# Loading v in f32 and narrowing it on chip, with a state update in two VectorE operations

## The chip, the cores and the metric

The kernel runs on one core of a Trainium2 chip. The metric is device time in microseconds (us) of a whole execution. Every experiment was run beside the kernel before on the same chip, in alternating rounds. The span of a profile is one execution and lies about 1.8 us under the time of the same run, so times are compared with times and spans with spans.

## The reference

A gated linear attention over 768 tokens (4 batches, 8 heads, 48 dimensions a head) is followed by a two-layer network with GELU:

```python
for t in range(S):                                   # S = 768
    state = alpha[:, :, t, :, None] * state + np.einsum('bhd,bhe->bhde', k[:, :, t], v[:, :, t])
    y[:, :, t] = np.einsum('bhd,bhde->bhe', q[:, :, t], state)
...
x = y.transpose(0, 2, 1, 3).reshape(B * S, H * D)    # 3072 x 384
out = gelu_tanh(x @ w_in) @ w_out                    # 384 x 2048, 2048 x 384
```

## The kernel before

It cuts the tokens into 6 chunks of 128 and works on *pairs*: one chunk of two batches, 12 pairs in all, numbered 0 to 11. For each pair it loads alpha (`a`), `q`, `k` and `v`. It takes the logarithm of alpha (`la`) and cumulative sums on TensorE (`cum`), scales q and k with exponentials of the sums (`qp`, `kp`), forms the attention products within the chunk (`at`), masks them (`atm`), multiplies them with v (`yps`), adds what the carried state gives, and updates the state (`kv`, `st`). Layer one (`hT`), GELU (`gT`) and layer two (`acc`) of earlier pairs fill TensorE in between.

v is narrowed to bf16 *by the load*, which GpSimd issues:

```python
def load(self, n, c, i, lo=0, hi=2):
    ...
        u[n] = self.tile(n, [C, 2, H, D], BF16 if n == "v" else F32)
        src = self.src[n][2 * i + lo:2 * i + hi].rearrange("b h s d -> s (b h) d")[c * C:(c + 1) * C]
        (nc.sync if e == "SP" else nc.gpsimd).dma_start(u[n][:, lo:hi]..., src)
```

The state is kept in pairs of heads, 128 partitions by 96 columns, of which two blocks of 64 by 48 are used. It is updated block by block:

```python
def carry(self, u, i, c, b):
    kv, old, new = u["kv", i], self.state[b][c % 2], self.state[b][(c + 1) % 2]
    for o in range(2):                                       # 64 partitions at a time
        ps, fs = slice(64 * o, 64 * o + 64), slice(D * o, D * o + D)
        acc = kv[ps, :, fs]
        if c > 0:
            ...
            nc.vector.tensor_tensor(s[ps], acc, old[ps, :, fs], op=ALU.add)
            acc = s[ps]
        nc.vector.tensor_tensor(new[ps, :, fs], acc, u["bend"][ps, i, :, None].to_broadcast(...), op=ALU.mult)
```

The order of the instructions on each engine is *planned* in Python when the kernel is built: every piece of work has a cost in a table `W`, a priority and dependencies, and a list scheduler fixes the order. Each engine then works through its list in order. Some entries of `W` stand for the time that a load takes to land. The first two pairs' alpha and q and the first pair's k go in small pieces over SyncE's and ScalarE's queues, the rest over GpSimd's:

```python
LOADS = ('gatea0', 'v0', 'gatek0', 'in 0', 'pk1', 'in 1', 'in 2', 'v1', 'in 3', 'out 0', 'out 1', '2a', ...)
RINGS = (..., ('a', 1, 0, 'SP'), ('a', 1, 1, 'SP'), ('a', 1, 2, 'SP'), ('a', 1, 3, 'SP'), ('q', 1, 0, 'SP'), ...)
```

A "gate" is a tiny GpSimd copy that waits for a piece, so that what follows in that queue starts later.

## Time and profile before

| | before |
|---|---|
| time, median of the runs ahead of the prediction | 185.78 us (184.66 to 186.07) |
| span of the profile | 183.2 us |
| TensorE, VectorE, ScalarE, GpSimd busy | 175.7, 104.2, 135.6, 60.9 us |
| first matmul of layer one | 17.2 us |

In this timeline the columns are start, duration, engine, line, operation, operands and count, and in brackets the idle time of the engine just before and what ended it:

```profile
10.64 0.66 PE L424 MATMUL at<-qkT 64*128 64x128 bf16 x16
11.11 2.48 DVE L431 TENSOR_TENSOR atm<-at,ut 128x512 bf16<-128x512 f32 x4 [0.82 <-PE at L424]
...
11.45 0.94 ACT L301 ACTIVATE la<-a 128x384 f16<-128x384 f32 x2 [0.76 <-DMA a<-in_alpha_dram]
12.02 0.82 PE L288 MATMUL cum<-la,ut_blk 128*128 128x384 f16 x7 [0.72 <-ACT la L301]
...
13.54 0.36 PE L473 MATMUL yps<-v,atm 128*128 128x48 bf16 x8
```

TensorE does pair 0's attention products (10.64 us) *before* it stops for pair 1's sums (12.02 us), which wait for alpha of pair 1.

### The profile page before, as it was taken

The page shows a single profiled execution, that of the slowest core. Times are in us where ns is not written, and L with a number is a line of the kernel's source. Part 1 is how long each engine was busy: PE and PEld are TensorE (multiplying, and loading weights), DVE is VectorE, ACT ScalarE, POOL GpSimd, SP SyncE. Part 2 cuts the span into 40 slices and gives each one's busy share as a digit, 9 for nine tenths or more (in the row PEclk, how much of TensorE's full clock was granted, in tenths as well). Part 3 has the DMA queues.
Part 4 walks back from the last instruction along what each step waited for, and adds up shares of the span by engine and source line. Part 5 has one row for each costly group of instructions (what it writes and reads, how often), then busy time and mean ns, then how long its engine had stood idle before and what let it go on. Part 6 is the DMA issues. An engine that isn't in the chain of part 4 may idle for free.

```text
span 183.2 us, 4630 instructions
## 1 busy us (share of the span) xinstructions
PE 175.7 (96%) x1861; PEld 129.3 (71%) x1861; DVE 104.2 (57%) x232; ACT 135.6 (74%) x310; POOL 60.9 (33%) x68
## 2 busy tenths in 40 slices
PE   7887999999999999999999999999999999999993
PEld 2465869666686787687688769678677677686873
DVE  7775954065969896597499798298644715000000
ACT  3666969873888789859799768899789884491941
POOL 2595837975545755564750200000000000000000
PEclk9999999999999999999999999999999999999999
DMA  5999999999999999999999955753271290311102
GB/s 155 187 242 211 187 231 214 204 202 174 195 281 183 169 229 197 181 225 205 180 213 235 179 171 100 104 115 67 52 170 46 43 202 4 88 43 47 43 0 86
DMA packets 51206, 27.76 MB, mean 151 GB/s; under 512 B 38833, under 2 KB 48241, under 8 KB 51185
## 3 DMA queue, kind: packets, MB, share of 16 engines
q0 software_dynamic: 32096, 17.70, 69.0%
q1 hardware_dynamic: 18512, 9.38, 21.5%
q10 hardware_dynamic: 576, 0.39, 0.7%
q8 instruction: 14, 0.23, 0.6%
q14 instruction: 8, 0.06, 0.1%
HBM read 25.17 MB, written 4.72 MB: 163 GB/s over the span
## 4 chain that ended last, share of the span: by engine, by line
PE 85%; DMA 6%; ACT 3%; DVE 2%; SPq 1%; ACTq 1%; issue 0%
PE acc L516 34%; PE hT L497 31%; PE at L424 4%; PE qkT_ps L364 4%; PE yps L473 3%; DMA a<-in_alpha_dram 2%; PE yps L470 2%; DMA q<-in_q_dram 2%; PE cum L320 2%; PE kv L441 2%; DMA qkT<-kp 2%; PE xT_ps L487 1%; DVE atm L431 1%; ACT L503 1%; PE cum L322 1%; SPq L247 1%
## 5 line engine op out<-in xcount | busy, mean ns | idle before, releaser
L497 PE MATMUL hT<-xT,w_in 128*128 128x256 bf16 x576 | 70.1, 273 | 0.4 <-ACT gT L503 0.4
L503 ACT ACTIVATE gT<-hT 128x256 bf16<-128x256 f32 x192 | 63.4, 387 | 8.6 <-PE hT L497 8.3
L516 PE MATMUL acc<-w_out,gT 128*128 128x384 bf16 (+1 forms) x400 | 68.8, 319 | 0.0
L497 PEld LDWEIGHTS <-w_in 128*128 128x128 bf16 x576 | 54.0, 98 | 8.0 <-issue 0.6
L516 PEld LDWEIGHTS <-gT 128*128 128x128 bf16 x400 | 36.8, 98 | 19.6
L431 DVE TENSOR_TENSOR atm<-at,ut 128x512 bf16<-128x512 f32 x48 | 30.9, 685 | 15.0 <-PE at L424 14.5
L354 DVE TENSOR_TENSOR qp<-q,b 128x768 bf16<-128x768 f32 (+1 forms) x15 | 11.7, 794 | 18.7 <-ACT b L343 15.8
L528 ACT COPY ot<-acc 128x384 f32<-128x384 f32 (+1 forms) x18 | 8.3, 462 | 13.9 <-PE acc L516 12.6
L235 POOL DMA_DIRECT2D v<-in_v_dram x13 | 14.6, 1123 | 9.6 <-PE hT L497 2.9
L235 POOL DMA_DIRECT2D k<-in_k_dram x11 | 12.2, 1112 | 11.0 <-DVE kp L354 5.2
L343 ACT ACTIVATE b<-cum 128x768 bf16<-128x768 f32 (+1 forms) x15 | 10.2, 684 | 6.7 <-PE cum L322 3.1
L235 POOL DMA_DIRECT2D q<-in_q_dram x11 | 12.3, 1114 | 7.0 <-DMA k<-in_k_dram 1.8
L235 POOL DMA_DIRECT2D a<-in_alpha_dram x11 | 12.3, 1114 | 5.9 <-ACT gT L503 2.2
L213 ACT ACT_TABLE_LOAD x9 | 11.5, 1283 | 2.8 <-issue 2.6
L480 ACT CAST x<-yps 128x384 bf16<-128x384 f32 x16 | 7.7, 481 | 7.8 <-PE yps L473 7.6
L458 DVE TENSOR_TENSOR st<-stmp,bend 64x192 bf16<-64x192 f32 x32 | 11.3, 353 | 1.5
L354 DVE TENSOR_TENSOR kp<-k,binv 128x768 bf16<-128x768 f32 (+1 forms) x15 | 11.8, 792 | 0.2
L456 DVE TENSOR_TENSOR stmp<-kv,st 64x192 f32<-64x192 f32 x32 | 11.3, 352 | 1.0 <-PE kv L441 0.7
L503 ACT ACT_TABLE_LOAD x9 | 11.5, 1283 | 0.2
L222 PE MATMUL idle<-zero 128*128 128x512 bf16 x27 | 9.5, 462 | 1.2 <-DVE blk L778 1.2
L382 DVE COPY qkT<-qkT_ps 128x1024 bf16<-128x1024 bf16 (+1 forms) x13 | 8.7, 688 | 3.0 <-PE qkT_ps L364 2.9
L343 ACT ACTIVATE binv<-cum 128x768 bf16<-128x768 f32 (+1 forms) x15 | 10.1, 683 | 0.0
(62 smaller groups left out, 159.4 us busy)
## 6 DMA issues: line engine op xcount, KB each, us to landing
out_dram<-ot SPq DMA_DIRECT2D x23, 192.0 KB, 2.3
a<-in_alpha_dram POOLq DMA_DIRECT2D x9, 384.0 KB, 13.1
q<-in_q_dram POOLq DMA_DIRECT2D x9, 384.0 KB, 13.2
k<-in_k_dram POOLq DMA_DIRECT2D x9, 384.0 KB, 13.3
v<-in_v_dram POOLq DMA_DIRECT2D x11, 192.0 KB, 13.3
w_in<-in_moe_w_in_dram POOLq DMA_DIRECT2D x4, 384.0 KB, 7.7
w_out<-in_moe_w_out_dram POOLq DMA_DIRECT2D x4, 384.0 KB, 9.8
a<-in_alpha_dram SPq DMA_DIRECT2D x6, 96.0 KB, 3.4
```

What stands on the lines that cost most here:

```text
L213: nc.scalar.add_instruction(mybir.InstLoadActFuncSet(name=nc.get_next_instruction_name(), act_func_set_id=i, engine=mybir.EngineType.Activ ...
L222: self.nc.tensor.matmul(ps, self.zero[:, 0:self.C], self.zero, start=True, stop=True)
L235: (nc.sync if e == "SP" else nc.gpsimd).dma_start(u[n][:, lo:hi].rearrange("t b h d -> t (b h) d"), src)
L343: self.nc.scalar.activation(u[n].rearrange("t i h d -> t i (h d)")[:, lo:hi], cum, AF.Exp, scale=1.0 if n == "b" else -1.0)
L354: self.nc.vector.tensor_tensor(out, rows, b, op=ALU.mult)
L382: self.copy(e)(t, ps)
L431: self.nc.vector.tensor_tensor(u["atm", i][:, o], u["at", i][o], self.ut[:, None, :].to_broadcast([self.C, self.H // 2, self.C]), op=ALU.mult)
L456: nc.vector.tensor_tensor(s[ps], acc, old[ps, :, fs], op=ALU.add)
L458: nc.vector.tensor_tensor(new[ps, :, fs], acc, u["bend"][ps, i, :, None].to_broadcast([64, H // 2, D]), op=ALU.mult)
L497: self.nc.tensor.matmul(h, self.w_in[:, j, nt * self.C:(nt + 1) * self.C], self.xT[c][:, j, lo:hi].rearrange("p g t -> p (g t)"), start=j ...
L503: return lambda e: self.nc.scalar.activation(self.gT[c % self.NG][:, nt, lo * self.C:hi * self.C], f.pop(("h", c, lo, nt)), AF.Gelu_apprx_ ...
L516: self.nc.tensor.matmul(f["acc", c, b][:, lo:hi], self.gT[c % self.NG][:, nt, b * self.C:(b + 1) * self.C], self.w_out[:, nt, lo:hi], star ...
```

## The change

Its intent: spare VectorE four instructions per update by doing two on all 128 partitions, with a decay that is zero outside the used blocks (one tiny multiply per pair makes it, `ends`). And take the narrowing of v out of the DMA engines, where it moves in 96-byte packets: v comes in f32, and GpSimd narrows it, VectorE for the first two pairs. The core of the diff:

```diff
-    qk2=910, ..., st=1400, st0=700, ...
+    qk2=910, ..., st=1090, st0=545, end=110, ...
-    ... cast=1500, ..., cast_0=1300, share=1200, cast_1=1900, ...
+    ... early_0=1000, share=1000, early_1=1400, vb1=300, vb2=550, vb1_pool=600, vb2_pool=950, ...
-    BUFS = dict(..., ot=6, bend=8, a=4, q=4, k=4, v=6)
+    BUFS = dict(..., ot=5, bend=3, ends=8, a=4, q=4, k=4, v=3, vb=4)
 ...
-                u[n] = self.tile(n, [C, 2, H, D], BF16 if n == "v" else F32)
+                u[n] = self.tile(n, [C, 2, H, D], F32)
 ...
+    def narrow(self, u, lo, hi):
+            ... (gpsimd or vector).tensor_copy(u["vb"][:, lo:hi], u["v"][:, lo:hi])
 ...
+            acc, old, new = u["kv", i], self.state[b][c % 2], self.state[b][(c + 1) % 2]
+            if c > 0:
+                nc.vector.tensor_tensor(s, acc, old, op=ALU.add)          # 128 x 384
+                acc = s
+            nc.vector.tensor_tensor(new, acc, ends, op=ALU.mult)          # 128 x 384
 ...
+                narrow[lo:hi] = [s.add("vb", {"DVE": W[f"vb{n}"]} if early else {"POOL": W[f"vb{n}_pool"]}, P + 9 if early else -1, ...)
```

Because the cost table changed, the whole order is planned anew as well.

More of the change, by code (lines that the diff above doesn't have):

```diff
@@ L17 @@
     cum=530, cum_packed=1500, t8=450, t4=225, attn=340, kv=170, inter=170, intra=205, tx=168, l1_4=655, l1_2=340, l2=655,
-    qk2=910, qk1=500, ev8=650, ev4=350, mask=640, st=1400, st0=700, xc=520, xe=330, ot=540,
+    qk2=910, qk1=500, ev8=650, ev4=350, mask=640, st=1090, st0=545, end=110, xc=520, xe=330, ot=540,
     ev8_act=960, ev4_act=520, xc_act=450, xe_act=450, ot_act=450,
-    strip=2120, cast=1500, weight=2080, dma=2100, issue=1100, wissue=760, sp=100, store=2600, turn=1250, landed=2200, xbar_qk=1500, xbar_x=1000, late_x=2500, piece=330, late_k=1500, piece_issue=450, begin=2700, cast_0=1300, share=1200, cast_1=1900, ln_packed=1040, cold=380, fill=216, zero=1100,
+    strip=2120, weight=2080, dma=2100, issue=1100, wissue=760, sp=100, store=2600, turn=1250, landed=2200, xbar_qk=1500, xbar_x=1000, late_x=2500, piece=330, late_k=1500, piece_issue=450, begin=2700, early_0=1000, share=1000, early_1=1400, vb1=300, vb2=550, vb1_pool=600, vb2_pool=950, ln_packed=1040, cold=380, fill=216, zero=1100,
 )
@@ L156 @@
     URGENT = (2,)
-    BUFS = dict(ca=1, yk=2, ff=4, la=3, qp=4, kp=4, b8=2, kn=2, qkT=4, atm=6, x=3, ot=6, bend=8,
-                a=4, q=4, k=4, v=6)
+    BUFS = dict(ca=1, yk=2, ff=4, la=3, qp=4, kp=4, b8=2, kn=2, qkT=4, atm=6, x=3, ot=5, bend=3, ends=8,
+                a=4, q=4, k=4, v=3, vb=4)
     def __init__(self, ctx, tc, q, k, v, alpha, w_in, w_out, out):
@@ L182, in __init__ @@
         self.ident = const.tile([C, C], BF16, name="ident")
+        self.half = const.tile([C, 2], F32, name="half")
         self.ones = const.tile([C, 1], F16, name="ones")
@@ L345, in exp, with emit @@
         return emit
+    def narrow(self, u, lo, hi):
+        def emit(e):
+            if "vb" not in u:
+                u["vb"] = self.tile("vb", [self.C, 2, self.H, self.D], BF16)
+            (self.nc.gpsimd.tensor_copy if e == "POOL" else self.nc.vector.tensor_copy)(u["vb"][:, lo:hi].rearrange("t b h d -> t (b h d)"), u["v"][:, lo:hi].rearrange("t b h d -> t (b h d)"))
+        return emit
     def scaled(self, u, n, lo, hi):
@@ L441, in emit, with ends @@
                 nc.tensor.matmul(kv[:, p, :], u["kn" if u["packed"] else "kp"][:, i, 2 * p:2 * p + 2, :].rearrange("t h d -> t (h d)"),
-                                 u["v"][:, i, 2 * p:2 * p + 2, :].rearrange("t h d -> t (h d)"),
+                                 u["vb"][:, i, 2 * p:2 * p + 2, :].rearrange("t h d -> t (h d)"),
                                  start=True, stop=True)
+        return emit
+    def ends(self, u):
+        C, H = self.C, self.H
+        def emit(e):
+            t = u["ends"] = self.tile("ends", [C, 2, H // 2, 2], F32)
+            (self.nc.gpsimd if e == "POOL" else self.nc.vector).tensor_tensor(
+                t.rearrange("f i p o -> f (i p) o"), u["bend"].rearrange("f i p -> f (i p)")[:, :, None].to_broadcast([C, H, 2]),
+                self.half[:, None, :].to_broadcast([C, H, 2]), op=ALU.mult)
         return emit
@@ L449, in emit @@
         def emit(e):
-            kv, old, new = u["kv", i], self.state[b][c % 2], self.state[b][(c + 1) % 2]
-            for o in range(2):
-                ps, fs = slice(64 * o, 64 * o + 64), slice(D * o, D * o + D)
-                acc = kv[ps, :, fs]
-                if c > 0:
-                    s = self.sb.tile([C, H // 2, D], F32, tag=f"stmp{o}", bufs=2, name="stmp")
-                    nc.vector.tensor_tensor(s[ps], acc, old[ps, :, fs], op=ALU.add)
-                    acc = s[ps]
-                nc.vector.tensor_tensor(new[ps, :, fs], acc,
-                                        u["bend"][ps, i, :, None].to_broadcast([64, H // 2, D]), op=ALU.mult)
+            acc, old, new = u["kv", i], self.state[b][c % 2], self.state[b][(c + 1) % 2]
+            if c > 0:
+                s = self.sb.tile([C, H // 2, 2 * D], F32, tag="stmp", bufs=2, name="stmp")
+                nc.vector.tensor_tensor(s, acc, old, op=ALU.add)
+                acc = s
+            ends = u["ends"][:, i].rearrange("f p o -> f (p o)")[:, :, None].to_broadcast([C, H, D])
+            nc.vector.tensor_tensor(new.rearrange("f p (o d) -> f (p o) d", o=2),
+                                    acc.rearrange("f p (o d) -> f (p o) d", o=2), ends, op=ALU.mult)
         return emit
@@ L472, in emit @@
             for h in range(H):
-                nc.tensor.matmul(y[:, h, :], u["atm", i][:, h % 2, h // 2, :], u["v"][:, i, h, :],
+                nc.tensor.matmul(y[:, h, :], u["atm", i][:, h % 2, h // 2, :], u["vb"][:, i, h, :],
                                  start=c == 0, stop=True, skip_group_check=True)
@@ L548, in load @@
             nonlocal n
-            land = W[{"v": "cast", "w": "weight"}.get(key[0], "strip")]
-            loads[key] = s.add("load", {"POOL": cost}, n, emit, gate, land=W[f"cast_{key[1]}"] if key[0] == "v" and key[1] in self.PACKED else land * 3 // 8 if key[0] != "w" and key[1] in self.SPLIT else land,
+            land = W[{"w": "weight"}.get(key[0], "strip")]
+            loads[key] = s.add("load", {"POOL": cost}, n, emit, gate, land=W[f"early_{key[1]}"] if key[0] == "v" and key[1] in self.PACKED else land * 3 // 8 if key[0] != "w" and key[1] in self.SPLIT else land,
                                late=W["share"] if key[:2] == ("v", 0) else 0)
@@ L599, in tasks @@
             early = m in self.EARLY
-            lns[m], ends[m], qp, kp, be = [], [], [None, None], [None, None], [None, None]
+            lns[m], ends[m], qp, kp, be = [], [], [None, None], [None, None], []
             cums, exps = [], []
@@ L611, in tasks @@
                 if u["sums"]:
-                    be[lo:hi] = [x[2]] * n
+                    be.append(x[2])
                 ends[m].append(x[-1])
@@ L644, in tasks @@
                 owner = every[0]
+            if u["sums"]:
+                end = s.add("end", {"DVE": W["end"]}, P + 16, self.ends(u), be)
+            narrow = [None, None]
+            for lo, hi in ((0, 1), (1, 2)) if early else self.parts(m):
+                n = hi - lo
+                narrow[lo:hi] = [s.add("vb", {"DVE": W[f"vb{n}"]} if early else {"POOL": W[f"vb{n}_pool"]}, P + 9 if early else -1, self.narrow(u, lo, hi),
+                                       [loads["v", m, lo]])] * n
+            loads["v", m, 0].take("v", *narrow)
             for j in range(2):
@@ L670, in tasks @@
                 y = s.add("y", {"PE": W["intra"] + (W["inter"] if c else 0)}, P + 20 + j, self.y(u, j, c, b),
-                          ms + turned + [loads["v", m, j]] + ([states[b, c - 1]] if c else []))
+                          ms + turned + [narrow[j]] + ([states[b, c - 1]] if c else []))
                 xc = s.add("x", {"ACT": W["xc_act"], "DVE": W["xc"]}, P + 20 + j, self.x(u, j), [y])
@@ L692, in tasks @@
                         backs.append(tb)
-                    kv = s.add("kv", {"PE": W["kv"]}, P + 30 + j, self.kv(u, j), [k, loads["v", m, j]])
+                    kv = s.add("kv", {"PE": W["kv"]}, P + 30 + j, self.kv(u, j), [k, narrow[j]])
                     st = states[b, c] = s.add("st", {"DVE": W["st" if c else "st0"]}, P + 30 + j, self.carry(u, j, c, b),
-                                              [kv, be[j]] + ([states[b, c - 1], ys[b, c - 1]] if c else []))
+                                              [kv, end] + ([states[b, c - 1], ys[b, c - 1]] if c else []))
                     kv.take("yk", st)
@@ L710, in tasks @@
             kp[0].take("kp", *tq, *kvs)
-            loads["v", m, 0].take("v", *vs)
+            narrow[0].take("vb", *vs)
             if u["sums"]:
-                be[0].take("bend", *cs)
+                be[0].take("bend", end)
+                end.take("ends", *cs)
         n = 0
@@ L778, in run @@
         nc.vector.memset(self.blk, 0.0)
+        nc.vector.memset(self.half, 0.0)
+        for o in range(2):
+            nc.vector.memset(self.half[64 * o:64 * o + 64, o:o + 1], 1.0)
         for t in self.ut_blk:
```

## The prediction

> **What bounds the kernel now.** I read the page's busy times first, then the busy tenths by slice, then windows, then the chain of waits, and last the groups.
>
> ```profile
> PE 175.7 (96%) x1861; PEld 129.3 (71%) x1861; DVE 104.2 (57%) x232; ACT 135.6 (74%) x310; POOL 60.9 (33%) x68
> ...
> PE   7887999999999999999999999999999999999993
> ...
> DMA  5999999999999999999999955753271290311102
> ...
> q0 software_dynamic: 32096, 17.70, 69.0%
> ```
>
> TensorE is busy 96% of the span, VectorE 57%, GpSimd 33%. The TensorE row is full from slice 5 on, the DMA row from slice 2 to 23: after the start TensorE looks like the bound, before it the loads. The windows (us, then busy us and count of PE, PEld, DVE, ACT, POOL; granted clock, DMA share, GB/s) give it by stage:
>
> ```profile
> 0.00:30.00 30.00, 26.01 (x278) 17.66 (x279) 21.33 (x71) 19.43 (x49) 18.70 (x31) 1.00 1.23 200
> 30.00:110.00 80.00, 79.60 (x901) 59.21 (x900) 56.06 (x115) 64.58 (x139) 42.22 (x37) 1.00 1.33 203
> 110.00:180.00 70.00, 69.85 (x691) 52.44 (x686) 26.85 (x48) 51.24 (x122) 0.00 (x0) 1.00 0.35 76
> ```
>
> Busy is not full speed, so I checked the rhythm. In the chain of waits 42 matmuls of layer one take 4.58 us (109 ns each) and 16 of layer two 2.60 us (162 ns each):
>
> ```profile
> 6.94 4.41 DMA a<-in_alpha_dram
> 11.34 0.02 issue
> ...
> 28.68 4.58 PE hT L497 x42
> 33.27 2.60 PE acc L516 x16
> ```
>
> Giving every matmul the median distance from its start to the next of its kind, I sum 155.4 us of wanted work, 7.1 us of filler on zeros and 16.3 us of gaps. Of fillers and gaps together (23.4 us) about 13.6 lie before 30 us and 9.9 after; 3.2 us follow the last matmul start. After 30 us only three gaps exceed 150 ns beyond that rhythm, 1.0 us in all, the largest 0.56 us beside a table load of ScalarE; the rest is switching between kinds of matmul. So after 30 us no load and no VectorE wait costs more than about 1 us. What can be won lies in the first 30 us.
>
> There the chain runs through transfers. The last piece of alpha of pair 1 lands at 11.34 us; the logarithm, the cumulative sums and the exponentials follow. The chain then goes to VectorE's multiply of q at 15.38 us, which the waits put down to a ScalarE copy that this multiply does not read. The trace has the last q piece of pair 1 landing at 15.26 us, so I take that as what held it. Behind it on VectorE are the copies of the turned x, and the first layer-one matmul starts at 17.21 us. The first v (issued 5.06 us) lands at 12.08 us, while these alpha and q pieces are under way.
>
> The groups that the change touches:
>
> ```profile
> L458 DVE TENSOR_TENSOR st<-stmp,bend 64x192 bf16<-64x192 f32 x32 | 11.3, 353 | 1.5
> L456 DVE TENSOR_TENSOR stmp<-kv,st 64x192 f32<-64x192 f32 x32 | 11.3, 352 | 1.0 <-PE kv L441 0.7
> ...
> L458 DVE TENSOR_TENSOR st<-kv,bend 64x192 bf16<-64x192 f32 x8 | 2.8, 355 | 0.8 <-ACT gT L503 0.7
> ...
> v<-in_v_dram POOLq DMA_DIRECT2D x11, 192.0 KB, 13.3
> ```
>
> They are VectorE work with almost no idle time before it, and nothing on TensorE waits long for it: the longest total of TensorE's weight loads behind stmp is 0.9 us in four waits.
>
> **What the Trainium skill says.** (1) "VectorE: DVE Perf Modes", section "The TRN2 errata", gives (N+151)/0.96 ns for an f32 tensor_tensor. For N=192 that is 357 ns (trace 352 to 355), for 384 it is 557 (the kp multiply 128x384: 552), for 768 it is 957 (952). It agrees, so the time follows the free size and half the partitions save nothing. (2) "GPSIMD Engine Reference", section "Elementwise — side-by-side cycle accounting", gives 1.03 cycles an element for a port-bound loop, at 1.2 GHz; the trace has only a one-element copy, 0.27 us at most, so a copy of 768 is estimated at 0.27+0.66=0.93 us, which no run here shows yet. (3) "SBUF — State Buffer", section "Who interferes with whom": a VectorE instruction with two SBUF inputs contends with a GpSimd instruction that reads SBUF. The trace before has no long GpSimd read to show it. (4) "DMA: Bandwidth & Descriptors", section "Queues, rings and completion order": each DMA engine alternates between queues by packets. The trace agrees at least that the two queues slow each other: the four alpha pieces of pair 0 land 0.2 to 0.7 us apart, those of pair 1, with v under way, 0.5 to 1.5.
>
> **The change part by part.**
>
> State update. Removed: 32+32+8 VectorE instructions of 64x192, 22.6+2.8=25.4 us. Added: 16 updates of two instructions 128x384 and 4 of one, at 552 ns: 36 x 0.552 = 19.9 us. Saved 5.5 us. Added too: one tiny multiply per pair for the masked decays (16 outputs, 0.17 us by the formula), 10 of them, 1.7 us, and about 0.2 us of memsets. Net 3.6 us less on VectorE. What the path sees: next to nothing, since TensorE is full where 16 of the 20 updates lie. I give it 0.1 us.
>
> Narrowing. VectorE gets four copies of 128x384 in the first two pairs; at two elements a cycle (384/2+150)/0.96 = 356 ns, 1.4 us in all. GpSimd gets nine copies of 768 and two of 384, about 9 x 0.93 + 2 x 0.6 = 9.6 us, on an engine busy 60.9 us, so about 70. VectorE's total should be 104.2 - 3.6 + 1.4 = 102. The copies of pair 0 stand near its four masks (11.1 to 13.6 us), before an idle stretch of 1.78 us; those of pair 1 fall in the busiest part. I charge 0.3 us to the path.
>
> The load. Bytes read from HBM stay; those written for v double, 2.36 MB more (27.76 to 30.1). Two opposite effects. Where the GpSimd queue is full the landings are 2.05 to 2.15 us after the one before for a, q and k, and about 1.45 (1.4 to 1.8) for v. An f32 v will take 2.1: 0.65 us more per pair, 6.5 us over pairs 2 to 11. But from pair 4 on alpha lands 9 us and more before its logarithm (pair 5: 57.1 against 72.4 us), so this is hidden; only pair 3, whose alpha lands at 40.19 us just as it is used, is close, and TensorE has other work then (9.8 of 10 us filled from 30 to 40).
> The other effect is in the packets. The narrowed v makes 24,576 packets of 96 B at 31 ns mean, 2048 per pair: 2048 x 31 / 16 = 4.0 us of every engine. f32 strips on the same queue travel in packets of about 4 KB, some 100 per strip, at 323 ns: 100 x 323 / 16 = 2.0 us. Packets therefore fall by 24,576 - 12 x 100 to about 27,800, and q0's share by some 24 us of 183, from 69% to about 56%. In the first 15 us this should let v0 and the q pieces beside it land 0.5 to 1.5 us earlier. I count 1.0 us, of which 0.2 is taken back by v1 standing ahead of the last quarter of w_in.
>
> Sum: -0.1 + 0.3 - 0.8 = -0.6 us, and another -0.3 us as a choice, for the smaller DMA occupancy next to weights and pair 2. 185.78 - 0.9 = 184.9.
>
> **The rivals.** First, VectorE is what matters, and 3.6 us less of it shortens the end, to about 182. Its slices reach 9 in places, and it has 8.7 of 10 us busy in 60 to 70; against it, TensorE has under 1 us of gaps there, most of it switching.
> Second, the loads become the bound between 20 and 45 us: v's extra 0.65 us for pairs 1 to 3 plus weights queued behind, 186.5 to 187. For it speak the full DMA row and pair 3's alpha; against it, only 0.15 us of TensorE gaps from 30 to 40.
> Third, GpSimd becomes a gate: its queue is in order, a narrowing that waits for its v (about 13 us from issue to landing) holds back the load issues behind it, and v has three buffers in place of six. If the planned order misses the landings, loads slip by a microsecond or two a pair: harmless while 9 us ahead, 187 to 189 if it happens at pairs 2 to 4.
> Fourth, the order that the kernel plans for itself is recomputed with other costs, so instructions move on every engine; that alone may shift the time a microsecond either way.
>
> **Range and chances.** Central 184.9 us. If the early win is the full 2 us: 183. If narrowings lie on the chain and the loads slip: 187. The range is 183.0 to 187.0. Faster by over 2% needs 182.1, more than I can find in the start: 0.07. Slower by over 2% needs 189.5, a gate early on GpSimd: 0.06. Within 2%: 0.87.
>
> **What would show it.** Right: TensorE still 96% or more; VectorE near 102 us; state instructions at 552 ns; packets near 27,800 and 30.1 MB; v landing about 2.1 us after its predecessor; GpSimd copies near 0.93 us; the first layer-one matmul near 16.4 us instead of 17.2, and the end earlier by about as much. Wrong: the same start but an earlier end (VectorE mattered); GpSimd long in wait on v with loads issued late; gaps on TensorE between 30 and 60 us behind loads or behind a narrowed v; a first matmul later than 17.2 us because the copies delay the masks or the x.

## The result, and the profile after

The changed kernel took 190.59 us (median of 4 runs, 189.12 to 191.15) against 185.22 us before (184.31 to 186.07). The ratio is 1.0276 with a 95% interval of 1.0204 to 1.0347: slower, and outside the predicted range of 183.0 to 187.0. Ratios here are the mean time of one kernel's fast runs over that of the other's fast runs of the same rounds, so not quite the ratio of the medians. The span of the profile grew from 183.2 to 189.4 us, by 6.2 us. The page of the changed kernel:

```profile
PE 178.2 (94%) x1864; PEld 130.3 (69%) x1864; DVE 105.2 (56%) x218; ACT 133.6 (71%) x305; POOL 69.1 (36%) x79
...
PE   7829999999899999999999999998999999999993
...
PEclk9996999999999999999999999999999999999999
...
DMA packets 27781, 30.11 MB, mean 159 GB/s; under 512 B 14256, under 2 KB 23664, under 8 KB 27760
...
q0 software_dynamic: 8672, 20.06, 47.6%
```

Packets, bytes and GpSimd are as predicted (27,800, 30.1 MB, about 70 us). The share of q0, the queue of GpSimd's loads, fell from 69.0 to 47.6% and not to the predicted 56; it is 62.6% in carry_only, a run told of below that keeps the old load of v, so part of the fall is not v's. But the third slice of TensorE, 9.5 to 14.2 us, has fallen from 8 to 2, and the granted clock (the share of TensorE's full clock that the profile shows) in the slice after it is 0.6. The windows, in the columns of the prediction:

```profile
0.00:30.00 30.00, 24.28 (x243) 15.63 (x244) 21.11 (x73) 17.31 (x42) 16.82 (x29) 0.94 1.03 212
30.00:110.00 80.00, 78.38 (x883) 58.68 (x882) 55.26 (x98) 60.68 (x132) 51.45 (x49) 1.00 0.93 223
```

In the first 30 us TensorE runs 243 matmuls where before it ran 278, and in the next 80 us it is idle 1.6 us where it was idle 0.4. A good clock for where the time goes is the start of the first GELU of each of the first three pairs' layer one, from the trace:

| first GELU of pair | 0 | 1 | 2 | last pair |
|---|---|---|---|---|
| before | 19.0 | 28.2 | 49.5 | 170.2 us |
| changed | 22.4 | 31.4 | 53.9 | 176.4 us |
| difference | 3.4 | 3.2 | 4.4 | 6.2 us |

So some 3.3 us are lost in the first 20 us, about 1.2 us between pairs 1 and 2, and 1.8 us later. The start, in the timeline of the changed kernel:

```profile
12.50 0.71 DVE L352 CAST vb<-v 128x384 bf16<-128x384 f32 x2 [1.61 <-DMA v<-in_v_dram]
...
13.60 0.94 ACT L302 ACTIVATE la<-a 128x384 f16<-128x384 f32 x2 [3.99 <-DMA a<-in_alpha_dram]
14.18 0.82 PE L289 MATMUL cum<-la,ut_blk 128*128 128x384 f16 x7 [3.69 <-ACT la L302]
...
15.81 1.03 PE L432 MATMUL at<-qkT 64*128 64x128 bf16 x16
...
16.46 2.48 DVE L439 TENSOR_TENSOR atm<-at,ut 128x512 bf16<-128x512 f32 x4 [0.27 <-PE at L432]
```

The logarithm of pair 1 starts at 13.60 us instead of 11.45, because alpha came late. On TensorE the sums of pair 1 now stand *ahead* of pair 0's attention products, so those, whose operands are ready by about 11 us, start at 15.81 us instead of 10.64. In the trace the pieces of alpha of pair 1 land at 8.08, 12.70, 13.11 and 13.50 us; before it was 8.35, 9.84, 10.29 and 11.34. The first v lands at 12.47 us, before at 12.08: it is not earlier, and three alpha pieces come right behind it.

The second place, in GpSimd's and then TensorE's timeline of the changed kernel:

```profile
44.85 1.15 POOL L236 DMA_DIRECT2D q<-in_q_dram  x1 [0.63 <-issue]
46.00 0.52 POOL L352 CAST vb<-v 128x384 bf16<-128x384 f32 x1
46.59 1.16 POOL L236 DMA_DIRECT2D k<-in_k_dram  x1
48.39 1.15 POOL L236 DMA_DIRECT2D a<-in_alpha_dram  x1 [0.65 <-ACT x L496]
49.54 0.52 POOL L352 CAST vb<-v 128x384 bf16<-128x384 f32 x1
```

```profile
48.96 0.33 PE L486 MATMUL yps<-st,qkT 128*128 128x96 bf16 x4
50.11 0.36 PE L489 MATMUL yps<-vb,atm 128*128 128x48 bf16 x8 [0.82 <-POOL vb L352]
```

The second half of pair 2's v landed at 37.19 us, but GpSimd narrows it at 49.54 us, 12 us later, because the loads ahead in its queue are issued only as earlier ones land. TensorE, in the middle of an otherwise full stretch, waits for it.

### The profile page after: what moved, and what is told of

Its sections match the earlier page's. It is cut to its first block, busy times and chain, and to the rows that moved or that the text cites. A ratio compares the mean times of both kernels' runs of the same rounds, so it can differ in the third digit from the quotient of the medians.

```text
span 189.4 us, 4622 instructions
## 1 busy us (share of the span) xinstructions
PE 178.2 (94%) x1864; PEld 130.3 (69%) x1864; DVE 105.2 (56%) x218; ACT 133.6 (71%) x305; POOL 69.1 (36%) x79
## 3 DMA queue, kind: packets, MB, share of 16 engines
q0 software_dynamic: 8672, 20.06, 47.6%
## 4 chain that ended last, share of the span: by engine, by line
PE 80%; DMA 7%; ACT 6%; issue 2%; DVE 2%; SPq 1%; ACTq 0%; POOL 0%; DVEq 0%
PE hT L513 30%; PE acc L532 29%; PE at L432 4%; DMA a<-in_alpha_dram 4%; PE qkT_ps L372 4%; PE yps L489 3%; ACT L519 2%; PE yps L486 2%; DMA q<-in_q_dram 2%; PE idle L223 2%; PE kv L449 2%; DMA qkT<-kp 1%; PE xT_ps L503 1%; PE cum L321 1%; ACT ot L544 1%
## 5 line engine op out<-in xcount | busy, mean ns | idle before, releaser
L439 DVE TENSOR_TENSOR atm<-at,ut 128x512 bf16<-128x512 f32 x48 | 30.9, 685 | 20.9 <-PE at L432 20.6
L362 DVE TENSOR_TENSOR qp<-q,b 128x768 bf16<-128x768 f32 (+1 forms) x15 | 12.4, 829 | 14.5 <-ACT b L344 14.5
L544 ACT COPY ot<-acc 128x384 f32<-128x384 f32 (+1 forms) x16 | 7.3, 459 | 17.5 <-PE acc L532 16.5
L236 POOL DMA_DIRECT2D a<-in_alpha_dram x11 | 12.2, 1111 | 14.5 <-ACT la L304 11.3
L352 POOL CAST vb<-v 128x768 bf16<-128x768 f32 (+1 forms) x11 | 8.6, 781 | 13.8 <-PE yps L489 13.8
L236 POOL DMA_DIRECT2D q<-in_q_dram x11 | 12.2, 1111 | 3.4 <-DMA w_out<-in_moe_w_out_dram 1.1
L236 POOL DMA_DIRECT2D k<-in_k_dram x11 | 12.2, 1110 | 3.2 <-DMA w_out<-in_moe_w_out_dram 1.1
L362 DVE TENSOR_TENSOR kp<-k,binv 128x768 bf16<-128x768 f32 (+1 forms) x15 | 12.4, 833 | 0.1
L223 PE MATMUL idle<-zero 128*128 128x512 bf16 x30 | 11.3, 483 | 1.2 <-DVE half L804 1.2
L496 ACT CAST x<-yps 128x384 bf16<-128x384 f32 x13 | 6.2, 478 | 7.8 <-PE yps L489 7.5
L390 DVE COPY qkT<-qkT_ps 128x1024 bf16<-128x1024 bf16 (+1 forms) x14 | 9.2, 688 | 2.0 <-PE qkT_ps L372 1.9
L496 DVE CAST x<-yps 128x384 bf16<-128x384 f32 x11 | 6.1, 554 | 7.3 <-PE yps L489 7.3
```

The costliest lines, as they stand in the source:

```text
L223: self.nc.tensor.matmul(ps, self.zero[:, 0:self.C], self.zero, start=True, stop=True)
L362: self.nc.vector.tensor_tensor(out, rows, b, op=ALU.mult)
L390: self.copy(e)(t, ps)
L439: self.nc.vector.tensor_tensor(u["atm", i][:, o], u["at", i][o], self.ut[:, None, :].to_broadcast([self.C, self.H // 2, self.C]), op=ALU.mult)
L496: self.copy(e)(x, u["y", i].rearrange("t h d -> t (h d)"))
L544: self.copy(e)(f["ot", c, b][:, sl], f["acc", c, b] if half is None else f["acc", c, b, half][:, sl])
```

## The experiments

The theory at this point (A): the loss comes from v in f32 and its narrowing, not from the new update; at the start, the f32 v crowds out alpha. The rivals: the new update or the order planned with its costs (B); the GpSimd narrowing (C). All medians below are of 4 to 6 fast runs (3 for v0_late); the kernel before had 184.65, 184.95 and 185.08 us. The changed kernel was not run again in them, so times of different calls are from different chips, and the ratio is the safer column.

| run | time, us | ratio to before (95%) | first GELU of pairs 0, 1, 2, last |
|---|---|---|---|
| changed kernel | 190.59 | 1.0276 (1.0204 to 1.0347) | 22.4, 31.4, 53.9, 176.4 |
| carry_only | 184.98 | 1.0020 (0.9973 to 1.0068) | 17.9, 27.0, 48.3, 169.9 |
| load_only | 192.47 | 1.0443 (1.0372 to 1.0514) | 23.8, 33.4, 58.8, 179.9 |
| early_cast | 189.46 | 1.0262 (1.0206 to 1.0318) | 18.3, 27.1, 53.3, 175.1 |
| at_first | 189.43 | 1.0237 (1.0180 to 1.0295) | 19.2, 28.3, 53.2, 175.2 |
| narrow_first | 185.92 | 1.0050 (1.0026 to 1.0074) | 18.7, 27.6, 49.2, 171.4 |
| narrow2_vec | 190.73 | 1.0292 (1.0239 to 1.0346) | 17.9, 27.3, 48.9, 175.6 |
| after_narrow2_vec | 189.24 | 1.0225 (1.0177 to 1.0274) | 21.9, 30.9, 52.4, 174.4 |
| v0_late | 190.78 | 1.0295 (1.0255 to 1.0334) | 23.9, 31.5, 53.0, 176.0 |
| both_orders | 187.36 | 1.0140 (1.0097 to 1.0183) | 19.7, 29.0, 50.5, 172.7 |
| v0_sync | 188.69 | 1.0198 (1.0154 to 1.0242) | 19.0, 30.5, 52.0, 173.5 |

All gave correct results.

Differences of a microsecond between these medians need care. In seven of the eleven kernels some runs have a mean clock of about 0.991 and the others 0.998 to 1.000, and the former took 0.9 to 1.9 us longer than the latter of the same kernel. In the profiled executions with such a mean, the clock stands at 0.50 for 3.4 us shortly after a long idle stretch of TensorE: in the changed kernel from 15.6 to 19.0 us, in early_cast from 46.3 to 49.7 us. So an idle stretch can cost more than its length, and a median depends on how many runs had such a spell.

**carry_only: the new update alone.** The kernel before with `carry`, `ends` and their costs from the changed kernel; loads untouched.

```diff
+            acc, old, new = u["kv", i], ...
+            nc.vector.tensor_tensor(s, acc, old, op=ALU.add)
+            nc.vector.tensor_tensor(new, acc, ends, op=ALU.mult)
-    st=1400, st0=700        (v: BF16 tile, narrowed by the load, stays)
+    st=1090, st0=545, end=110
```

> The kernel before with the new state update alone (two VectorE operations on 128 partitions and the small multiply for the masked decays), v still narrowed by the load. Theory A (the loss of 5.4 us is in the load of v and its narrowing): within 1 us of the kernel before, 184.2 to 186.2, first layer-one matmul near 17.2 us as before, alpha of pair 1 landed by 11.5 us. Rival B (the new update or the order planned anew with its costs is what costs): 188 us or more. VectorE busy near 102 us on either.

It took 184.98 us, the same as before. VectorE's total fell to 100.8 us; the groups of its operations on VectorE (busy us, mean ns, then idle before):

```profile
L467 DVE TENSOR_TENSOR st<-stmp,ends 128x384 bf16<-128x384 f32 x16 | 8.9, 558 | 0.5
L464 DVE TENSOR_TENSOR stmp<-kv,st 128x384 f32<-128x384 f32 x16 | 8.8, 549 | 0.4 <-PE kv L442 0.4
```

Rival B is out. So is any hope in the saved 3.4 us of VectorE: they bring nothing, as TensorE did not wait for VectorE. (Its trace gains 1.2 us by pair 2, which are nearly gone at the end. Two gaps of TensorE behind GELU, 0.17 us up to 109.1 us and 0.61 us up to 123.2, stand in this order and, as 0.18 and 0.61 us, in the changed kernel's, and not in the order before.)

**load_only: the load and the narrowing alone.** The changed kernel with the old `carry`, the old `bend` and the old costs 1400 and 700.

```diff
-            nc.vector.tensor_tensor(new, acc, ends, op=ALU.mult)      # and the add on 128 partitions
+            for o in range(2): ...                                    # two blocks of 64, as before
-    st=1090, st0=545, end=110
+    st=1400, st0=700
```

> The changed kernel with the old state update: only the f32 load of v and the narrowing on chip. Theory A: the whole loss is here, 189.5 to 191.5 us, last alpha piece of pair 1 landing near 13.5 us instead of 11.3, first layer-one matmul near 21 us. Rival B: within 1.5 us of the kernel before, under 187.

It took 192.47 us, the whole loss and 1.9 us on top, 1.0 us above the range given. The last alpha piece of pair 1 landed at 13.69 us. TensorE waited 0.4 us and 2.0 us for the two narrowings of pair 2. What the 1.9 us are is not shown: all four runs had a mean clock of 0.991 or less, and in the profile the loads of the steady stretch landed 2.1 us apart, as in the kernel before, and not 1.8 us as in the changed kernel.

**early_cast: v of pairs 0 and 1 narrowed by the load again.** Ten pairs stay in f32.

```diff
+                u[n] = self.tile("vb" if v and c == 0 else n, ..., BF16 if v and c == 0 else F32, n)
-            for lo, hi in ((0, 1), (1, 2)) if early else self.parts(m):      # narrow
+            for lo, hi in () if early else self.parts(m):
-    early_0=1000, share=1000, early_1=1400
+    early_0=1300, share=1200, early_1=1900
```

> The changed kernel, with v of the first two pairs again narrowed by the load (no VectorE narrowing); the other ten pairs stay f32 with GpSimd narrowing, the new update stays. Theory A, in its early form (v0 in f32 crowds out alpha of pair 1 in the first 14 us): 3 to 4 us less than the changed kernel, 186.5 to 187.5, first layer-one matmul near 17.2 us; what stays over the kernel before, 1 to 2.5 us, would be the GpSimd narrowing gating TensorE at 49 us (0.98 us there) and the planned order. If the later GpSimd work is the main cost instead (rival C): 189 us or more.

189.46 us: a miss, and inside the range of rival C (189 or more). The start was cured as expected (first matmul of layer one at 16.46 us; first GELU 18.3 instead of 22.4; alpha by 11.02 us). But the edit changed two things there: with the old costs of the first loads of v, the planned order also went back to pair 0's attention products first, so this run cannot tell the late alpha from the order behind it:

```profile
10.61 0.66 PE L437 MATMUL at<-qkT 64*128 64x128 bf16 x16
...
11.70 0.82 PE L291 MATMUL cum<-la,ut_blk 128*128 128x384 f16 x7 [0.43 <-ACT la L304]
```

Only 1.1 us came of the cure, not 3 to 4. The 4 us were given back at once, as TensorE's timeline shows:

```profile
42.58 0.34 PE L491 MATMUL yps<-st,qkT 128*128 128x96 bf16 x4
45.48 0.36 PE L494 MATMUL yps<-vb,atm 128*128 128x48 bf16 x8 [2.56 <-POOL vb L357]
```

TensorE came to pair 2's product with v 4.2 us earlier than in the changed kernel (42.6 against 46.8 us) and stood there. The narrowings of pair 2 start at 44.9 and 48.8 us here, at 46.0 and 49.5 us in the changed kernel: almost a fixed date. The spell of half clock from 46.3 us follows this wait of 2.56 us. So theory A, in its early form, named one of two holds, and the second hides most of the first.

**at_first: one planned order.** In the changed kernel, pair 1's sums must come after pair 0's attention products on TensorE.

```diff
-    URGENT = (2,)
+    URGENT = (0, 2)
-                cums[0].deps += ats[m - 1]
+                for t in cums:
+                    t.deps += ats[m - 1]
```

> The changed kernel with one planned order forced: TensorE's cumulative sums of pair 1 come after both attention products of pair 0, as they did before. Loads are untouched, so alpha of pair 1 still lands near 13.5 us. If the planned order (sums of pair 1 ahead of pair 0's products, in order on TensorE) makes the late alpha costly: 1.5 to 3 us less than the changed kernel, 187.5 to 189, first layer-one matmul near 18.5 us. If the late alpha alone sets the start: no change, 190 to 191.

189.43 us, 0.4 us above what the first theory gave and under what its rival gave. The first GELU came at 19.2 us, 3.2 us earlier, although the last alpha piece still landed late, at 12.78 us (13.50 in the changed kernel, 11.34 before). So the late alpha costs most of what it does through what stood *behind* it in TensorE's queue: with the products ahead of the sums, the first GELU is 0.9 us later than early_cast's, not 4.1. Again the date of pair 2's narrowing (45.2 and 48.8 us) took most of the gain: TensorE's gaps there are 1.81 and 1.26 us, where the changed kernel has only the one of 0.82.

This called for a new theory (D): GpSimd's in-order queue is the second hold. Its copies wait behind load issues, and an issue waits until an earlier load has landed. The rival (E): the copies cost by their work or by contention with VectorE.

**narrow_first: the copies of pair 2 ahead in GpSimd's queue.** On the base of early_cast, so with a good start.

```diff
+            if m == 2:
+                for x in range(4, 12):
+                    for r in "aqkv":
+                        loads[r, x, 0].deps += narrow
```

> The kernel with v of the first two pairs narrowed by the load, plus one planned order: GpSimd narrows v of pair 2 before it issues any load of pairs 4 to 11. The narrowing stays on GpSimd. Theory D (GpSimd's narrowing of pair 2 stands behind load issues that wait for room among the transfers under way, so it comes at 45 and 49 us instead of right after its v has landed): the narrowings start before 38 us, no gap of TensorE behind them, and 4 to 5 us less than without the order, 184.5 to 186. Rival E (the GpSimd copies cost by their own work or by contention with VectorE): little change, 188 to 190.

185.92 us, 3.5 us less than early_cast (4 to 5 were expected), with the same eleven copies on the same engine. GpSimd's timeline:

```profile
34.44 1.15 POOL L238 DMA_DIRECT2D v<-in_v_dram  x1
35.58 1.37 POOL L357 CAST vb<-v 128x384 bf16<-128x384 f32 x2
36.91 1.16 POOL L238 DMA_DIRECT2D a<-in_alpha_dram  x1
...
49.78 0.85 POOL L357 CAST vb<-v 128x768 bf16<-128x768 f32 x1
```

The copies are done by 37 us, and no gap of TensorE behind a narrowing is left. Rival E is out as the main cause. The 0.5% that stay over the kernel before are above the noise (interval 1.0026 to 1.0074).

**narrow2_vec: pair 2's copies on VectorE instead.** Same base.

```diff
-                ... {"DVE": W[f"vb{n}"]} if early else {"POOL": W[f"vb{n}_pool"]}, P + 9 if early else -1, ...
+                ... {"DVE": W[f"vb{n}"]} if early or m == 2 else {"POOL": W[f"vb{n}_pool"]}, P + 9 if early or m == 2 else -1, ...
```

> The same base, with the two narrowings of pair 2 on VectorE instead of GpSimd, nine of ten GpSimd copies left in place. Theory D: as the reordered one, 184.5 to 186. Rival E: nine copies of eleven are left, so most of the loss stays, 188 to 189.5.

190.73 us (188.95 in its one run at full clock): a miss of what theory D was made to say, and by the number alone a point for E. The trace shows otherwise. Pair 2 was cured (its first GELU at 48.9 us), and the hold moved to pair 3, whose v had landed at 44.77 us and was narrowed at 55.7 us, with TensorE waiting:

```profile
52.97 0.40 PE L437 MATMUL at<-qkT 64*128 64x128 bf16 x8
56.62 0.33 PE L454 MATMUL kv<-vb,kp 128*128 128x96 bf16 x4 [3.24 <-POOL vb L357]
```

In narrow_first, where loads wait for the copies, pair 3's copy came at 49.8 us. The theory held; what I had left out was that the next copy stands in the same queue.

**after_narrow2_vec: the changed kernel with that move.** The same two edits on the changed kernel, early v in f32.

```diff
+                ... if early or m == 2 else {"POOL": W[f"vb{n}_pool"]} ...   # on the changed kernel
```

> The changed kernel (v of the first two pairs in f32, too) with only the narrowings of pair 2 moved to VectorE. If the late start (first GELU of pair 0 at 22.4 us against 17.9 with the cast load) and the gate at pair 2 overlap rather than add, the start alone stays: 4 to 4.5 us over the update-only kernel, 189 to 189.5. If the two add: 186.

189.24 us, as "overlap" had it. The start stays (first GELU at 21.9 us), and pair 3's copy, at 55.5 us, is no gate, since a late TensorE does not come to it before. The two holds are not a sum: each alone makes most of the loss.

**v0_late: the first v only after alpha of pair 1.** On top of the last one.

```diff
-    LOADS = ('gatea0', 'v0', ...
+    LOADS = ('gatea1', 'v0', ...
```

> As the last one, with the first v issued only after the last alpha piece of pair 1 has landed. If the f32 v under way is what holds those pieces back (they landed at 12.7 to 13.5 us, right behind v at 12.5): the last one lands by 10.5 us, earlier than the 11.3 of the kernel before. The first v then lands near 13 to 14 us, so the first GELU near 19.5 to 20.5 and the time 186.5 to 188. If the pieces are late for another reason: still 12 us or later.

The landing settled its question: the four alpha pieces land at 8.07, 8.56, 8.90 and 9.33 us, so v under way is what holds them back. The time, 190.78 us, is a miss. Issued at 10.05 us, the v landed at 17.76 us, not at 13 to 14: with 7.7 us from issue to landing it takes as long as in the changed kernel, and pair 0's products with v wait for it.

**both_orders: the changed kernel with only the two orders altered.** The edits of at_first and narrow_first together; every load and every copy stays.

```diff
+    URGENT = (0, 2)      # and the loop over cums
+                        loads[r, x, 0].deps += narrow
```

> The changed kernel whole (v in f32 for all pairs, narrowed on VectorE for two pairs and on GpSimd for ten, new update) with only two planned orders altered: TensorE's sums of pair 1 behind the attention products of pair 0, and GpSimd's narrowing of pair 2 ahead of the loads of pairs 4 to 11. If the loss is a matter of two in-order queues and not of the added work or bytes: about 4 us less than the changed kernel, 186 to 187; third GELU block near 50 us (53.9 in the changed kernel, 48.3 with the update alone). If the added copies and bytes cost by themselves: 188.5 or more.

187.36 us, 3.2 us less than the changed kernel and 0.4 us above the range I gave. By the ratios, each to the kernel before on the same chip, 1.4 of the 2.8% are gone, or 2.5 us. So half of the loss or a little more, 2.5 to 3.2 us, is a matter of what stands behind what in two in-order queues. The 2.3 us that stay over the kernel before are mostly the start: the second GELU block begins 2.0 us later than in carry_only, with alpha of pair 1 still landing at 12.21 us.

**v0_sync: a try for a version that beats both.** carry_only with the first v alone in f32, on SyncE's queue between alpha and q of pair 1, narrowed on VectorE.

```diff
-    RINGS = (..., ('a', 1, 3, 'SP'), ('q', 1, 0, 'SP'), ...)
+    RINGS = (..., ('a', 1, 3, 'SP'), ('v', 0, 0, 'SP'), ('q', 1, 0, 'SP'), ...)
-    LOADS = ('gatea0', 'v0', ...
+    LOADS = ('gatea0', ...
```

> The kernel before with the new update, and only the first v in f32, issued on SyncE's queue between the alpha and the q pieces of pair 1 and narrowed on VectorE; all other v as before. Meant as a version that could beat both: alpha of pair 1 last lands near 9.4 us (as where v was held back), v by 11 to 12, q by 14, so the first GELU near 17 us against 17.9 to 19.0, and 183.5 to 184.5 us. If an f32 v costs as much on this queue, the q pieces land at 15 us or later and the time is 185 to 187.

188.69 us, a miss of both ranges. Alpha landed by 9.46 us and v at 11.78 us, as hoped, but the q pieces behind it came at 15.65 to 18.68 us. The delay had only been passed on. No version tried beats the kernel before; carry_only equals it.

## Why the prediction was wrong

*What bounds the kernel* was right, and it is why the update brought nothing: after 30 us TensorE has no slack to give, and only the start could be won. Two of the signs of being wrong that the prediction listed came: a first matmul of layer one later than 17.2 us (21.21), though not because copies delayed the masks or the x, and a gap of TensorE behind a narrowed v (0.82 us at 50.1 us).

*State update*: predicted 3.6 us less VectorE work and 0.1 us on the path; carry_only measured 3.4 us less and no change.

*Narrowing*: GpSimd's copies were put at 0.93 us and took 0.84; the engine's total was put at 70 and came to 69.1. VectorE was put at 102 and came to 105.2 us. Part of that is contention: the multiplies of 128x768 took up to 1.26 us (q) and 1.57 us (k) beside GpSimd's copies, and 0.96 us at most in carry_only. The path was charged 0.3 us for all the copies. **This is one step that failed**, and not by their length: the copy is short, but it stands in a queue. The prediction named it, as the third rival ("GpSimd becomes a gate ... 187 to 189 if it happens at pairs 2 to 4"), and gave it little weight because alpha lands 9 us ahead of its use from pair 4 on. That was the wrong margin. What counts is when GpSimd *reaches* the copy, and that could be read in the profile before. From 40 us on its load issues are about 2 us apart with waits between them, while each issue costs 1.15 us. The kernel's own plan, which knows no such waits, puts pair 2's copies at 31.2 and 35.6 us; they ran at 46.0 and 49.5 us. Before, only loads stood in that queue, most of them needed much later, so its lag was free. Not tested is the share of the f32 v's three buffers in place of six: in the changed kernel's profile GpSimd stands idle for 2.0 us in all before five loads of v, each just behind a copy.

*The load*: predicted -0.8 us, from earlier landings in the first 15 us. **This is the step that failed by sign:** the first GELU came 3.4 us later. The packets came out as worked out, but engine time per packet did not tell when a load lands. The first v landed 0.4 us later, and alpha of pair 1, which shares the engines with it, 2.2 us later. The other profiles bear out the alpha and not the v: in five with a first v narrowed by the load, v landed at 11.6 to 12.7 us and the last alpha piece at 11.0 to 11.8; in five with it in f32 at the same place in the queue, v at 11.2 to 12.5 and alpha at 12.2 to 13.7. The last q piece, which I took for the holder of the start, came at about the same time (14.99 against 15.26 us). And the fourth rival, the order planned anew, was worth more than the "microsecond either way" that I gave it: it put the waiting sums ahead of ready work, and at_first gets 3.2 us of the start back by that alone.

The hidden part, v's extra 0.65 us per pair, was right in kind, and harmless. The profiled executions differ in the pace of all their loads, whatever the form of v: alpha, q and k land 2.1 us apart in the kernel before and in load_only, 1.8 us in carry_only and in the changed kernel. At the first pace v went from about 1.45 to 2.1 us, as predicted, at the second from 1.4 to 1.8.

What stays open is how the f32 v holds back the alpha pieces. The last three land right behind v, 0.2 to 0.6 us apart, in every run with a first v in f32 under way on GpSimd's queue. Two mechanisms fit: large packets that take the engines' turns, or completions that stand behind v's. The Trainium skill, "DMA: Bandwidth & Descriptors", section "Queues, rings and completion order", says that a semaphore's increment lands only after every earlier write from that engine, across its queues; that would fit the landings, but no run here separates the two. The traces narrow it: a landing is the last of 16 increments of the load's semaphore, and of the last alpha piece the eighth came at 10.59 us both before and after, the sixteenth at 11.34 and 13.50 us. So the load as a whole is not late: five of its 16 increments are, those that come after 11.34 us. The granted clock is not the main cause. In the profile TensorE does nothing for 3.7 us up to 14.18 us, and the clock falls to 0.5 from 16 to 18 us, which agrees with "TensorE: Matmul & The Clock Gate", section "Part 1", on an idle window of about 3.4 us. (A shorter stretch, 2.56 us in early_cast, was followed by it too.) But of the four runs two had a mean clock of 1.00 (189.12 and 190.73 us) and two of 0.991 (190.46 and 191.15 us), and all four lie above every run of the kernel before.

## What to carry to other kernels

Ahead of moving work to an engine with idle time, ask where in that engine's queue it will stand and what the entries in front of it wait for: an engine that issues loads can be idle two thirds of the time and still be a dozen microseconds behind its plan. When one hold is cured and little comes of it, look for a second one with a fixed date right behind it, and judge each cure by where TensorE stands at several points in time, not by the total alone. And on in-order engines a late transfer costs what was put behind it, so the order is worth checking before the transfer is.

## What the Trainium skill lacked or had wrong

- "DMA: Bandwidth & Descriptors" has nothing on how many loads from GpSimd can be under way. In the changed kernel an issue of the steady stretch begins about 0.3 us after a landing, with six other loads still under way (46.59 after a landing at 46.28 us, 48.39 after 48.09), so issues go at the pace of landings, 1.8 us here and 2.1 us in the kernel before.
- The same page says that a cast in the DMA goes through GpSimd's queue, but not what it costs. Here the narrowing load of v landed about 1.45 us after its predecessor where an f32 load of the same elements took about 2.1, although its 24,576 packets of 96 B take 31 ns each (carry_only: 1.4 against 1.8).
- "GPSIMD Engine Reference", section "Elementwise — side-by-side cycle accounting": the rate of 1.03 cycles an element holds. A copy from f32 to bf16 took 0.84 us for 768 and 0.52 us for 384, so 0.82 ns an element, 0.99 cycles at the page's 1.2 GHz. The estimate of 0.93 us was 10% high by its fixed part, 0.27 us from a one-element copy in the trace, where these two sizes leave 0.21 us.
- "SBUF — State Buffer", section "Who interferes with whom", agrees: VectorE's multiplies with two SBUF inputs took up to 1.26 us (q) and 1.57 us (k) beside GpSimd copies, against 0.96 us at most in carry_only. The longest small multiply of the decays, 0.80 us against 0.17, lies beside a load issue of GpSimd and not beside a copy; its cause is not shown.
- "TensorE: Matmul & The Clock Gate", section "Part 1", puts the fall to half clock after an idle window of about 3.4 us; in early_cast it fell after 2.56 us, in narrow2_vec after 3.24 us, each time for 3.4 us.
